# Moving the loads of the second expert behind its rows at the start of the expert stage

## The chip, the cores and the metric

The kernel runs on one core of a Trainium2 chip. That core has a matrix engine (TensorE, PE in the profile), a vector engine (VectorE, DVE), a scalar engine (ScalarE, ACT), a general engine (GpSimd, POOL) and a queue engine (SyncE, SP), which issues most of the transfers between the chip's large memory (HBM) and the on-chip memory. Each engine works through its own list of instructions in order and waits for the others at semaphores. The metric is the time of one execution on the device in microseconds (us); the times shown are medians of several runs of the same kernel.

## The reference

The reference computes three stages one after the other, in float32:

```
# 1. attention: batch 4, heads 8, sequence 576, head size 64
scores = q @ k.T / sqrt(64) + min(-(cum_i - cum_j), 0)   # cum: running sum of max(s, 0); causal mask
x = softmax(scores) @ v                                   # reshaped to 2304 rows of 512

# 2. mixture of experts: 8 experts, inner size 1024, one expert for each row
idx  = argmax(cosine(x, expert_emb) / tau)                # which expert a row goes to
gate = softmax(...)[idx]                                  # a row's own gate weight
out[idx == e] = gate * (max(x[idx == e] @ w1[e], 0) @ w2[e])

# 3. a gated product on all rows: inner size 1536
y = ((out @ w_a) * (out @ w_b)) @ w_out
```

Which expert a row goes to is known only once attention and routing are done.

## The kernel before, in words

Every matrix product is made of three products of float32r values: a number is split into a high part (a cast) and a low part (the number less its high part), and high by high, high by low and low by high are added up. So each weight block goes through a split after it has been loaded: ScalarE casts two halves (line 273, through `hi_op`), and VectorE and GpSimd subtract one half each (line 281, `lo_op`).

**Routing.** During attention each finished group of 128 rows is scattered by an indirect transfer of GpSimd (line 1046) into a buffer `xs` in HBM, where every expert has its own stretch of rows. The unused end of a stretch is zeroed by `zfill(e)` (line 1359, one transfer from `zrow`, issued at line 1257), and `xload(e)` (line 1364) fetches an expert's rows into the tile `xg` with two transfers (lines 1374 and 1375; for the first expert three, line 1372). `xs` is one tile to the framework: a fetch waits until the zeroing before it is done, and a zeroing waits until the fetch before it is done. There is one `xg` buffer.

**Expert stage.** Experts are taken in turn, e = 0 to 7, and each in eight steps f = 0 to 7. Step (e, f) (`products`, line 1592) makes the 128 hidden columns f (12 matmuls into the bank `h`, line 1553), and after them the share that step f - 1 has in the four output banks `y` (12 matmuls, line 1578). Behind the first of these, ScalarE makes the high part `hh` with the relu (line 1561) and VectorE the low part `hl` (line 1562); the second reads both one step later. From step 3 on, three transposes a step (`xtr`, line 1390, matmuls at line 1397) turn a quarter of the next expert's rows, for which these have to be there. At an expert's end `yout` (line 1585) copies the four banks to `mx` tiles and stores them to `yt` in HBM.

**Weights.** An expert has eight blocks of 512 KB, written here as (e, 0) to (e, 7): four of `w1` and four of `w2`. `wload2` (line 1423) issues the next block's load on SyncE, `wsplit2` (line 1429) splits the oldest loaded one. They are called at the end of each step, so that on ScalarE the casts of a step stand between the `hh` of this step and that of the next. Blocks (0, 0) to (0, 6) are loaded during attention.

**The passage from attention to the experts** (lines 1750 to 1775) is the place of the change. SyncE, after (0, 4) to (0, 6), issues the load of (0, 7); the counts of rows are read; the first expert's rows are fetched; meanwhile TensorE repeats matmuls with an unused result (`idle`, line 1754; its two counts are `WARM[2]` and `WARM[6]`), VectorE and GpSimd make the low parts of (0, 4) to (0, 6), and two of five small pieces of the gate weights (`misc`: m1 to m5, lines 1477 to 1511) are computed. Then come `zfill(1)`, three more loads, the transposes of the first expert's rows (`xtr0`, line 1377: eight for columns up to 256, four for the rest, each into a bank that ScalarE and VectorE have to have read), and the loop of steps. In it `xload(1)` stands in step (0, 1), and this step has two splits and two loads.

The order is that of the source text: within this part of the program nothing reorders the instructions of an engine. What SyncE waits for holds back every transfer behind it.

**Third stage.** `abmm(i, f)` (line 1633) makes 128 columns of both products of a group of 384 rows. ScalarE copies one to an `mx` tile (line 1649), VectorE multiplies it by the other (line 1654). `omm` (line 1688) makes the output products. `mx` tiles come from a pool of four (`mxp`, line 1342), which `yout` uses too. The last expert's `yout` falls between `abmm(0, 0)` and `abmm(0, 1)`.

Of the kernel before, what the change touches and what calls it, by code (L numbers as in the profile page):

```python
# [18 lines left out]
B, H, S, D = 4, 8, 576, 64  # L19
# [13 lines left out]
FIRST = float(1 << 20)  # L33
TICKS = (1, 1, 2)
PEND = (10, 1, 1)
WARM = (30, 84, 2, 0, 20, 10, 3)
LAT = 140.0
GATE = 3000.0
DRAIN = 93.0
# [1 line left out]
DEP = mybir.DependencyInfo(mybir.DependencyClass.Sync, mybir.DependencyReason.DATA)  # L41
# [103 lines left out]
def moe_kernel(tc, q, k, v, s, emb, tau, w1, w2, wa, wb, wo, out, dbg=None):  # L145
    nc = tc.nc
# [3 lines left out]
    left, right = ExitStack(), ExitStack()  # L150

    def pool(st, n, b, **kw):
        return st.enter_context(tc.tile_pool(name=n, bufs=b, **kw))
# [28 lines left out]
    with left, right:  # L182
# [38 lines left out]
        slots = {}  # L221
# [7 lines left out]
        def slot_src(e, j):  # L229
            return w1_src(e, j) if j < 4 else w2_src(e, j - 4)  # L230
# [6 lines left out]
            nslot[0] += len(spare)  # L237
            return (spare[0] if spare and x < 62 and (x + 3) % 5 > 2 else stage).tile(shape, dtype, name=nm, tag="st")

        def slot_load(src):  # L240
            t = slot([128, 1024], F32, "st")
            d = t if len(src.shape) == 2 else t.rearrange("p (a c) -> p a c", a=src.shape[1])
            nc.sync.dma_start(out=d, in_=src)
            return t

        def slot_load64(src):
# [32 lines left out]
        def lo_op(eng, t, o, a, b):  # L279
            e = nc.vector if eng == "D" else nc.gpsimd  # L280
            e.tensor_tensor(out=o[:, 1, a:b], in0=t[:, a:b], in1=o[:, 0, a:b].bitcast(F32), op=ALU.subtract)  # L281
# [7 lines left out]
        if True:  # L289
# [773 lines left out]
            wstate, wtok = {}, {}  # L1063
# [275 lines left out]
            gp = pool(mo, "gp", 1)  # L1339
            spare.append(pool(mo, "spare", 2))  # L1340
            hp = pool(right, "hp", 2, side="right")
            mxp = pool(right, "mxp", 4, side="right")
            keep = pool(right, "keep", 1, side="right")
            pos = keep.tile([128, NT], U32, name="pos")
            pd = keep.tile([128, NT, 2], F32, name="pd")
# [7 lines left out]
            def who(e):  # L1353

                if e not in pes:
                    pes[e] = nc.sync.value_load(ci[:1, 3, e:e + 1], min_val=0, max_val=E - 1) if e else 0
                return pes[e]
# [19 lines left out]
            def xtr0():  # L1377
                t = xhs[0] = [xhp.tile([128, 4, GT], F32R, name=x)[:, :, :CAPS[0]] for x in ("xh", "xl")]
                for a0, a1 in ((0, 256), (256, CAPS[0])):
                    for d in range(4):  # L1380
                        for a in range(a0, a1, 128):
                            nc.tensor.transpose(
                                out=yb[d][:, a:a + 128], in_=xgs[0][:, a // 128, 128 * d:128 * d + 128], identity=ident
                            )
                        nc.scalar.copy(out=t[0][:, d, a0:a1], in_=yb[d][:, a0:a1])
                        nc.vector.tensor_tensor(
                            out=t[1][:, d, a0:a1], in0=yb[d][:, a0:a1], in1=t[0][:, d, a0:a1].bitcast(F32), op=ALU.subtract
                        )

            def xtr(e, d):  # L1390
                if d == 0:
# [28 lines left out]
            def ringpool(nm):  # L1420
                return ringa0 if nm in ("w0", "w1", "w2", "w3") else rings[nm] if nm in rings else ringa1[0] if nm[0] == "w" else rings[nm[0]]

            def wload2():
                if loaded[0] < len(jobs):
                    key = jobs[loaded[0]][0]
                    stg[key] = slot_load(slot_src(who(key[0]), key[1]))
                    loaded[0] += 1

            def wsplit2():
# [325 lines left out]
                for x in range(n):  # L1755
                    warm((hb + yb)[x % 6], w[:, :128], w[:, :512], 1)

            wload2()
            idle(WARM[2])
            most = nc.values_load(cov[:1, 0:1], min_val=-CAP, max_val=N)  # L1760
            overflow()
# [2 lines left out]
            who(1)  # L1764
            idle(WARM[6])
            count(0)
            for j in range(4, 7):
                for x in range(2):
                    lo_op("DG"[j == 6], wstate[j], slots[0, j], 512 * x, 512 * x + 512)
            for _ in range(2):  # L1770
                misc.pop(0)()
            zfill(1)
            for _ in range(3):
                wload2()
            xtr0()
            prev = None
            for e in range(E):
                for f in range(8):
                    if f == 5 and e + 1 < E:
                        count(e + 1)  # L1780
                    products(e, f, prev)
                    prev = (e, f)
                    if (e, f) == (0, 1):
                        xload(1)
                    if (e, f) == (1, 0) or f == 7 and 0 < e < E - 2:
                        xload(e + 2 - (f == 0))
                    if (e, f) == (E - 2, 7):
                        yload(0)
                    if f == 4 and e + 2 < E:
                        zfill(e + 2)  # L1790
                    if 3 <= f < 7:
                        if e + 1 < E:
                            xtr(e + 1, f - 3)
                        else:
                            ysplit(0, f - 3)
                    if e == E - 1 and f == 7:
                        yload(1)
                    for _ in range(2 if (e, f) == (0, 1) else 1):
                        wsplit2()
                        wload2()  # L1800
                    if e == E - 2 and f >= 4:
                        vload()
                    if e == E - 1:
                        for _ in range(TICKS[0] if f not in (4, 6) else 0):
                            tick(5 if f < 4 else 3)
                    if misc and (e or f > 1):
                        misc.pop(0)()
# [74 lines left out]
```

## Time and profile before

| | |
|---|---|
| median of 3 runs | 956.17 us (954.9 to 956.58) |
| the profiled execution: its own time | 953.78 us |
| the profiled execution: span of the core | 952.1 us |
| TensorE busy | 917.8 us, 96% of the span |
| VectorE, ScalarE, GpSimd busy | 54%, 45%, 27% |
| mean granted clock of TensorE (profiled execution) | 0.994 of 2.4 GHz |
| transfers | 107.90 MB, mean 113 GB/s |

The span runs from the first to the last instruction in the trace; the execution's own time is 1.7 us longer, and the median of the runs 2.4 us longer than that. All clock times below count from the start of the span. A row of a timeline merges like instructions that follow each other: start, time until the last of them ends, engine, line, operation, destination and source; in square brackets the engine's idle time before it, and what ended that. Matmuls overlap in the pipeline, so the single times of a row add up to more than it lasts. The granted clock is 1.00 at 2.4 GHz and 0.50 at 1.2 GHz.

### The profile page before, as it was taken

The numbers are of one execution on the slowest core, as the hardware profiler recorded it, in microseconds if no ns is written. First come the engines' busy times: TensorE is split into PE (matmuls) and PEld (weight loads), VectorE is DVE, ScalarE is ACT, GpSimd is POOL, SyncE is SP. The second block draws the span as 40 slices with busy tenths as digits, with TensorE's granted clock in tenths as the row PEclk, the third lists the DMA queues.
The fourth block names the chain that finished last, engine by engine and source line by source line (L and its number), as shares of the span: only waits on it lengthen the run. The fifth ranks groups of instructions, "written<-read, shape, count | busy, mean of one in ns | idle before, by whom it ended". The sixth has DMA issues, their size and how long they took to land.

```text
span 952.1 us, 17669 instructions
## 1 busy us (share of the span) xinstructions
PE 917.8 (96%) x6447; PEld 839.7 (88%) x6448; DVE 516.9 (54%) x1319; ACT 432.0 (45%) x1074; POOL 256.4 (27%) x308
## 2 busy tenths in 40 slices
PE   8998999999889999999999999999999999999996
PEld 7777878777669999999998999999999999999995
DVE  8788888798756343455678888732212222222112
ACT  6677888876645444455544434421211111121111
POOL 6122323256234333344303344632001001001001
PEclk9999999999999999999999999999999999999999
DMA  5774555526277667677736444412010010000000
GB/s 136 175 154 105 143 116 123 140 71 185 96 221 241 225 193 218 215 226 241 223 106 204 129 118 131 90 26 75 1 34 34 1 34 34 1 1 34 1 1 34
DMA packets 102259, 107.90 MB, mean 113 GB/s; under 512 B 58445, under 2 KB 72733, under 8 KB 102157
## 3 DMA queue, kind: packets, MB, share of 16 engines
q1 hardware_dynamic: 98573, 97.04, 36.0%
q0 software_dynamic: 3552, 9.46, 2.8%
q8 instruction: 65, 1.06, 0.5%
q14 instruction: 37, 0.30, 0.1%
q10 hardware_dynamic: 32, 0.04, 0.0%
HBM read 77.90 MB, written 20.44 MB: 103 GB/s over the span
## 4 chain that ended last, share of the span: by engine, by line
PE 68%; DMA 2%; DVE 0%; issue 0%; SPq 0%; POOLq 0%; ACT 0%; DVEq 0%; ACTq 0%
PE h L1643 16%; PE x L1643 16%; PE y L1664 14%; PE y L1578 10%; PE h L1553 10%; DMA xg<-xs 1%; PE x L1397 1%; PE x L1664 1%; PE h L1664 1%; DMA xs<-zrow 1%; DMA yt<-mx 0%; DVE xl L1631 0%; SPq L1372 0%; POOLq L1878 0%; DVE mx L1654 0%
## 5 line engine op out<-in xcount | busy, mean ns | idle before, releaser
L1654 DVE TENSOR_TENSOR mx<-x,mx 128x384 f32<-128x384 f32 x72 | 39.9, 555 | 225.1 <-PE x L1643 225.0
L1655 ACT CAST hh<-mx 128x384 fp32r<-128x384 f32 x71 | 36.4, 512 | 159.0 <-DVE mx L1654 159.0
L1649 ACT COPY mx<-h 128x384 f32<-128x384 f32 x72 | 34.5, 479 | 150.8 <-PE h L1643 149.8
L1683 POOL DMA_INDIRECT out_dram<-mx,pmt x18 | 17.6, 979 | 292.5 <-DVE mx L1682 223.2
L653 ACT ACTIVATE z<-z,mn 128x192 f32<-128x192 f32 (+3 forms) x128 | 78.2, 611 | 37.9 <-DVE mn L647 37.2
L1643 PE MATMUL h<-xh,w 128*128 128x384 f32 x288 | 79.8, 337 | 1.3 <-ACT mx L1649 1.3
L1643 PE MATMUL h<-xh,v 128*128 128x384 f32 x288 | 79.7, 337 | 0.0
L1643 PE MATMUL x<-xh,w 128*128 128x384 f32 x288 | 78.9, 334 | 0.0
L633 PE MATMUL st<-KS,QS 128*128 128x288 f32 (+3 forms) x160 | 58.7, 374 | 9.4 <-DVE mn L647 7.4
L756 PE MATMUL pt<-ident,z 128*128 128x128 f32 x448 | 63.5, 277 | 3.3 <-ACT pT L180 1.6
L281 POOL TENSOR_TENSOR w<-st,w 128x512 fp32r<-128x512 f32 (+1 forms) x43 | 47.1, 1101 | 68.1 <-ACT w L273 57.8
L647 DVE CUSTOM_DVE_ANT_0 z<-st,maskb 128x192 f32<-128x192 f32 (+3 forms) x128 | 58.7, 477 | 9.5 <-PE st L636 7.3
L1562 DVE SCALAR_TENSOR_TENSOR hl<-h,hh 128x288 fp32r<-128x288 f32 (+6 forms) x64 | 31.2, 487 | 58.8 <-ACT hh L1561 58.8
L1656 DVE TENSOR_TENSOR hl<-mx,hh 128x384 fp32r<-128x384 f32 x71 | 39.7, 559 | 41.1 <-ACT hh L1655 41.1
L800 PE MATMUL xa<-pT,vn 128*64 128x128 f32 x896 | 60.0, 278 | 1.9 <-ACT pT L180 1.6
L281 POOL TENSOR_TENSOR v<-st,v 128x512 fp32r<-128x512 f32 x32 | 43.2, 1353 | 62.5 <-ACT v L273 48.7
L1664 PE MATMUL y<-v,hh 128*128 128x512 f32 x192 | 59.8, 392 | 0.0
L756 PEld LDWEIGHTS pt<-ident,z 128*128 128x128 f32 x448 | 49.9, 141 | 11.0 <-ACT z L653 4.3
L1553 PE MATMUL h<-xh,v 128*128 128x256 f32 (+2 forms) x256 | 59.0, 304 | 0.0
L1578 PE MATMUL y<-hh,v 128*128 128x256 f32 (+2 forms) x256 | 58.0, 300 | 0.0
L1553 PE MATMUL h<-xh,w 128*128 128x288 f32 (+3 forms) x256 | 57.8, 302 | 0.0
L800 PEld LDWEIGHTS xa<-pT,vn 128*64 128x64 f32 x896 | 47.9, 137 | 11.0 <-issue 5.6
(308 smaller groups left out, 2520.0 us busy)
## 6 DMA issues: line engine op xcount, KB each, us to landing
st<-in_moe_w_dram SPq DMA_DIRECT2D x64, 512.0 KB
QS<-sp SPq DMA_DIRECT2D x62, 128.0 KB
st<-in_moe_w_a_dram SPq DMA_DIRECT2D x12, 512.0 KB
st<-in_moe_w_b_dram SPq DMA_DIRECT2D x12, 512.0 KB
st<-in_moe_w_out_dram SPq DMA_DIRECT2D x12, 512.0 KB
xg<-yt SPq DMA_DIRECT2D x6, 768.0 KB
xg<-xs SPq DMA_DIRECT2D x7, 512.0 KB
kn<-in_k_dram SPq DMA_DIRECT2D x24, 128.0 KB
```

The source lines that it names most:

```text
L281: e.tensor_tensor(out=o[:, 1, a:b], in0=t[:, a:b], in1=o[:, 0, a:b].bitcast(F32), op=ALU.subtract)
L633: nc.tensor.matmul(st[:m, :wp], lhsT=qs[:, h, s0 - 64:s0 - 64 + m], rhs=ks[:, h, c0:c0 + wp], start=True, stop=False)
L647: nc.vector.tensor_tensor_reduce(out=z[:m, h, c0:c0 + w], in0=st[:m, :w], in1=maskb[:m, S - kk + c0:S - kk + c0 + w], op0=ALU.add, op1=ALU ...
L653: nc.scalar.activation(out=z[:m, h, :kk], in_=z[:m, h, :kk], func=AF.Exp, scale=-1.0, bias=m1, accum_out=rsum[:m, tid(b, c), 2 * p + h:2 * ...
L756: nc.tensor.transpose(out=pt[:, 128 * x:128 * x + 128], in_=zs[i][:, h, a0:a0 + 128] if c else z0s[u % 2], identity=ident)
L800: nc.tensor.matmul(xa[64 * h:64 * h + 64, :m], lhsT=v_[:m, 2 * p + h, :], rhs=locs[i][bk, h], start=bk == 0, stop=bk == c,)
L1553: nc.tensor.matmul(ph[:, :n], lhsT=w[:, hl, 128 * f:128 * f + 128], rhs=mv[:, d, :n], start=k_ == 0, stop=k_ == 11,)
L1578: nc.tensor.matmul(ys[e][d][:, :n], lhsT=w[:, hl, c0 + 128 * d:c0 + 128 * d + 128], rhs=mv[:, :n], start=f == 0 and k_ == 0, stop=f == 7 a ...
L1643: nc.tensor.matmul(p, lhsT=w[:, hl, d, c0:c0 + 128], rhs=mv[:, d, :], start=d == 0 and k_ == 0, stop=d == 3 and k_ == 2,)
L1654: nc.vector.tensor_tensor(out=g, in0=pp[1], in1=g, op=ALU.mult)
L1656: nc.vector.tensor_tensor(out=gl, in0=g, in1=gh.bitcast(F32), op=ALU.subtract)
L1664: nc.tensor.matmul(ots[i][t], lhsT=st[:, 128 * t:128 * t + 128], rhs=w[:, hl, c0:c0 + 512], start=f == 0 and k_ == 0, stop=f == 11 and k_ ...
```

## The change

There are four edits; the loads of the first two steps are laid out anew with the first and the third.

- The load of (0, 7) moves from ahead of the passage to behind the call of `xtr0`, and gets a wait of its own: it is issued once the ninth transpose of the first expert's rows (the first of the second group) is done. `zfill(1)` stands behind it. Only one more load, (1, 0), is issued ahead of the loop instead of three.
- The `idle` counts go from 2 and 3 to 1 and 2. Piece m3 of the gate weights (an exponential with its table load on ScalarE) joins m1 and m2 in the passage, and so m4 and m5 move up a step. The low parts of (0, 5) go from VectorE to GpSimd.
- `xload(1)` moves from step (0, 1) to step (0, 0). In step (0, 0) there is one split and two loads, in step (0, 1) two of each; after it the loads stand three blocks ahead of the splits, where it was four.
- The pool of `mx` tiles grows from four to five.

```
-WARM = (30, 84, 2, 0, 20, 10, 3)
+WARM = (30, 84, 1, 0, 20, 10, 2)
...
-        def slot_load(src):
+        def slot_load(src, after=None):
...
-            nc.sync.dma_start(out=d, in_=src)
+            x = nc.sync.dma_start(out=d, in_=src)
+            if after:
+                tc.add_manual_dep(x.ins, after, DEP, reason="rows first")
...
-            mxp = pool(right, "mxp", 4, side="right")
+            mxp = pool(right, "mxp", 5, side="right")
...
+                        if a0 and d == 0:
+                            first = x.ins.name
+                return first
...
-            wload2()
             idle(WARM[2])
...
-            for j in range(4, 7):
+            for x in range(2):
+                lo_op("D", wstate[4], slots[0, 4], 512 * x, 512 * x + 512)
+            for _ in range(3):
+                misc.pop(0)()
+            for j in (5, 6):
                 for x in range(2):
-                    lo_op("DG"[j == 6], wstate[j], slots[0, j], 512 * x, 512 * x + 512)
-            for _ in range(2):
-                misc.pop(0)()
+                    lo_op("G", wstate[j], slots[0, j], 512 * x, 512 * x + 512)
+            turned = xtr0()
+            wload2(turned)
             zfill(1)
-            for _ in range(3):
-                wload2()
-            xtr0()
+            wload2()
...
-                    if (e, f) == (0, 1):
+                    if (e, f) == (0, 0):
                         xload(1)
...
-                    for _ in range(2 if (e, f) == (0, 1) else 1):
-                        wsplit2()
+                    for x in range(2 if e == 0 and f < 2 else 1):
+                        if f or x == 0:
+                            wsplit2()
                         wload2()
```

What stands on SyncE in a row, before: from the zeroing of the second expert's rows (`xs<-zrow`) to the end of the fetch of its rows (`xg<-xs`). The four loads `st<-in_moe_w1` are the blocks (1, 0) to (1, 3); `ISA` rows work out an address.

```order
L1257 DMA xs_95<-zrow_270 736x1x256
L1537 UNCONDITIONAL_BRANCH x3
L243 ISA
L243 DMA st_4885<-in_moe_w1_dram 128x1024
L243 ISA
L243 DMA st_4887<-in_moe_w1_dram 128x1024
L243 ISA
L243 DMA st_4889<-in_moe_w1_dram 128x1024
L243 ISA
L243 DMA st_4955<-in_moe_w1_dram 128x1024
L1374 ISA
L1374 DMA xg_5010<-xs_95 128x2x512
```

And now, at the same place on SyncE: the first load is block (0, 7), which waits for the ninth transpose; the two loads `st<-in_moe_w1` are (1, 0) and (1, 1).

```order
L243 DMA st_4911<-in_moe_w2_dram 128x2x512
L1259 ISA
L1259 DMA xs_95<-zrow_270 736x1x256
L1542 UNCONDITIONAL_BRANCH x3
L243 ISA
L243 DMA st_4914<-in_moe_w1_dram 128x1024
L1376 ISA
L1376 DMA xg_4945<-xs_95 128x2x512
L1377 ISA
L1377 DMA xg_4945<-xs_95 112x512
L243 ISA
L243 DMA st_4953<-in_moe_w1_dram 128x1024
```

The zeroing now has the load of (0, 7) ahead of it, and the load of (1, 1) now stands behind the fetch of the rows, which waits for the zeroing.

What stands on ScalarE in a row, before, from the relu of step (0, 0) to that of step (0, 3) (`hh`); the casts `w7`, `v0`, `v1`, `v2` are the splits of (0, 7), (1, 0), (1, 1), (1, 2), and the table load with `lt` is m3.

```order
L1561 ACTIVATE hh_4946<-h0_4631 128x352
L273 CAST w7_4950<-st_4637 128x512 x2
L1537 UNCONDITIONAL_BRANCH
L1561 ACTIVATE hh_5006<-h1_4632 128x352
L1537 UNCONDITIONAL_BRANCH
L273 CAST v0_5013<-st_4885 128x512 x2
L273 CAST v1_5020<-st_4887 128x512 x2
L1561 ACTIVATE hh_5076<-h0_4631 128x352
L273 CAST v2_5080<-st_4889 128x512
L1537 UNCONDITIONAL_BRANCH
L273 CAST v2_5080<-st_4889 128x512
L1488 ACT_TABLE_LOAD
```

And now, the same piece on ScalarE:

```order
L1566 ACTIVATE hh_4941<-h0_4631 128x352
L275 CAST w7_4948<-st_4911 128x512 x2
L1542 UNCONDITIONAL_BRANCH
L1566 ACTIVATE hh_5006<-h1_4632 128x352
L1542 UNCONDITIONAL_BRANCH
L275 CAST v0_5010<-st_4914 128x512 x2
L275 CAST v1_5017<-st_4953 128x512 x2
L1566 ACTIVATE hh_5073<-h0_4631 128x352
L275 CAST v2_5077<-st_4955 128x512
L1542 UNCONDITIONAL_BRANCH
L275 CAST v2_5077<-st_4955 128x512
L1566 ACTIVATE hh_5137<-h1_4632 128x352
```

The table load has left this place; the casts of (1, 1) stand ahead of the relu of step (0, 2), as they did.

## Rows read from the trace of the kernel before

**Rows 1.** The page, part 1: busy time of each engine

```profile
PE 917.8 (96%) x6447; PEld 839.7 (88%) x6448; DVE 516.9 (54%) x1319; ACT 432.0 (45%) x1074; POOL 256.4 (27%) x308
```

**Rows 2.** Waits of TensorE from 285 on: us in total, times, longest

```profile
PE h L1643 <- ACT mx L1649: 1.3, 1, 1.3
PE x L1397 <- DMA xg<-xs: 0.3, 1, 0.3
```

**Rows 3.** The chain that ended last, 240 to 330: start, us, what

```profile
266.21 3.38 DMA xg<-xs
...
269.80 6.20 DMA xs<-zrow
...
276.73 8.23 DMA xg<-xs
```

**Rows 4.** Timeline of TensorE, and of its weight loads (PEld), in the passage

```profile
269.27 0.75 PEld L1382 LDWEIGHTS y<-ident,xg 128*128 128x128 f32 x7 [0.67 <-DMA xg<-xs]
...
270.57 1.32 PE L1382 MATMUL y<-ident,xg 128*128 128x128 f32 x4 [0.31 <-DVE xl L1386]
...
281.26 0.30 PE L1578 MATMUL y<-hh,w 128*128 128x288 f32 x1
...
284.27 0.41 PE L1397 MATMUL x<-ident,xg 128*128 128x128 f32 x2 [1.25 <-DMA xg<-xs]
...
285.12 0.39 PE L1553 MATMUL h<-xh,w 128*128 128x288 f32 x1
```

**Rows 5.** Timeline of SyncE, the issue of transfers

```profile
234.94 9.45 SPq L243 DMA_DIRECT2D st<-in_moe_w_dram  x3
...
270.67 4.64 SPq L243 DMA_DIRECT2D st<-in_moe_w_dram  x4
276.11 0.39 SPq L1374 DMA_DIRECT2D xg<-xs  x1
```

**Rows 6.** Timeline of ScalarE in the passage

```profile
269.68 2.48 ACT L1385 CAST xh<-y 128x256 fp32r<-128x256 f32 x8 [6.75 <-issue]
...
279.19 1.14 ACT L273 CAST v<-st 128x512 fp32r<-128x512 f32 x2 [0.37 <-DMA st<-in_moe_w_dram]
280.24 0.46 ACT L1561 ACTIVATE hh<-h 128x352 fp32r<-128x352 f32 x1
...
281.74 1.28 ACT L1488 ACT_TABLE_LOAD   x1
```

**Rows 7.** Timeline of VectorE and of GpSimd in the passage

```profile
280.73 0.53 DVE L1562 SCALAR_TENSOR_TENSOR hl<-h,hh 128x352 fp32r<-128x352 f32 x1
...
275.13 1.30 POOL L281 TENSOR_TENSOR w<-st,w 128x512 fp32r<-128x512 f32 x1 [11.27 <-ACT w L273]
```

**Rows 8.** Transfers, 250 to 300: how much the zeroing moves

```profile
xs<-zrow SPq DMA_DIRECT2D x1, 736.0 KB
```

**Rows 9.** Windows: stretch, length, PE busy, granted clock, DMA share, GB/s

```profile
271.00:272.00 1.00, 1.00 (x5) 1.00 0.78 172
272.00:273.00 1.00, 1.00 (x10) 1.00 0.92 187
...
276.00:277.00 1.00, 1.00 (x10) 1.00 0.98 385
```

**Rows 10.** Windows, the same columns, around two waits of TensorE

```profile
262.00:264.50 2.50, 0.00 (x0) 1.00 0.04 10
...
265.00:268.00 3.00, 3.00 (x5) 0.50 0.59 158
...
283.00:284.20 1.20, 0.03 (x1) 1.00 1.05 265
```

**Rows 11.** Timelines behind the last expert's stores: ScalarE, TensorE, VectorE

```profile
502.47 0.48 ACT L1649 COPY mx<-h 128x384 f32<-128x384 f32 x1 [1.07 <-DMA yt<-mx]
...
503.00 0.44 PE L1643 MATMUL h<-xh,w 128*128 128x384 f32 x1 [1.25 <-ACT mx L1649]
...
503.44 0.55 DVE L1654 TENSOR_TENSOR mx<-x,mx 128x384 f32<-128x384 f32 x1
```

More of the change, by code (lines that the diff above doesn't have):

```diff
@@ L1381, in xtr0 @@
                         for a in range(a0, a1, 128):
-                            nc.tensor.transpose(
+                            x = nc.tensor.transpose(
                                 out=yb[d][:, a:a + 128], in_=xgs[0][:, a // 128, 128 * d:128 * d + 128], identity=ident
@@ L1421, in ringpool, with wload2 @@
                 return ringa0 if nm in ("w0", "w1", "w2", "w3") else rings[nm] if nm in rings else ringa1[0] if nm[0] == "w" else rings[nm[0]]
-            def wload2():
+            def wload2(after=None):
                 if loaded[0] < len(jobs):
                     key = jobs[loaded[0]][0]
-                    stg[key] = slot_load(slot_src(who(key[0]), key[1]))
+                    stg[key] = slot_load(slot_src(who(key[0]), key[1]), after)
                     loaded[0] += 1
```

## The prediction

> **What bounds the kernel now.** Read the busy times first: TensorE is busy 96% of the span, the next engine 54% [rows 1]. So an edit pays only where TensorE stands still, and costs only where it makes TensorE stand still. The waits of TensorE name the places: from 285 us to the end there are two rows, 0.3 us for the second expert's rows and 1.3 us behind a copy of ScalarE [rows 2]; the expert stage is otherwise a closed row of matmuls. The chain of waits shows what leads up to the first place: the first expert's rows land 3.38 us after the last of their three issues, at 269.59; then the zeroing, issued at 269.80, takes 6.20 us, to 276.00; then the second expert's rows take from 276.73 to 284.96 [rows 3]. The timeline of TensorE has the stall itself: the product y of step (0, 2) starts at 281.26 and lasts about 1.6 us, the three transposes stand at 284.27 behind 1.25 us of idle time, and step (0, 4) starts at 285.12 [rows 4]. About 2.1 us go there.
>
> Now see how near another wait lies. The casts of block (1, 1) start at 279.19, held by their load (0.37 us of idle time before them); behind them come hh of step (0, 2), from 280.24 [rows 6], and hl, from 280.73 for 0.53 us, to 281.26 [rows 7]. That is when TensorE starts the y that reads them [rows 4]. It did not wait, but there was nothing to spare: whatever makes block (1, 1) later makes this y later by the same.
>
> **Part by part.**
>
> *Load of (0, 7).* Before, it is the third of the three issues that end at 244.39 [rows 5], 20 us ahead of anything that needs the queue: it cost nothing there. Now it waits for the ninth transpose, which starts at 270.57 [rows 4]; with 0.33 us for it (four such steps in 1.32 us) SyncE goes on at 270.9. The zeroing, issued at 269.80 before, comes after this issue (0.39 us for one, as that of the rows [rows 5]) and its own address, at about 271.5: 1.7 us later. The transfers add to that. The 736 KB of the zeroing [rows 8] go at 187 GB/s, though four loads were issued from 270.67 on, and the loads come behind it at 385 GB/s [rows 5, 9]: SyncE's transfers run one behind the other, so 512 KB ahead of the zeroing hold it for 524,288 B / 385 GB/s = 1.4 us. Its data took 753,664 B / 187 GB/s = 4.0 of its 6.20 us; with the transfer engines 0.78 busy in the window from 271 to 272 and 0.92 in the next [rows 9] they began near 271.1, 1.3 us after the issue, which leaves 0.9 us from the last byte until it is told done. Then (0, 7) moves from 270.9 + 1.3 = 272.2 to 273.6, the zeroing from 273.6 to 277.6, and it is done at 278.5, 2.5 us later than before. Bounds: +1.7 (issue alone) to +3.0.
>
> *Rows one step sooner.* The fetch used to stand behind four loads, now behind one, but its wait is the zeroing, which was the last to end before too. Issues at 278.6 and 279.2 (0.1 and 0.7 after the zeroing, as before). About 1.3 us later it moves, 736 KB (the second expert's 368 rows of 2 KB) at 265 GB/s [rows 10], 2.8 us, to 282.7, and lands near 283.3. TensorE would want the rows at 282.9: this wait is all but gone.
>
> *What is late next.* All that stood ahead of the fetch stands behind it: SyncE in its wait holds (1, 1), (1, 2), (1, 3). Block (1, 1) is issued at 279.7, moves behind the rows from 282.7 to 284.1 and, with 0.9 us to be told done, can be cast at 285.0, against 279.19: +5.8. By the chain above y of step (0, 2) then starts at 281.26 + 5.8 = 287.1, TensorE idle since 281.3. Add 1.6 us for y and 0.3 for the transposes (their rows are there): step (0, 4) starts at 289.0 against 285.12, **+3.9 us**. Bounds: with the zeroing only 1.7 later, (1, 1) issued at 278.9, and 3.4 us from issue to landing (the rows of the first expert from their last issue [rows 3]), the cast is at 282.3 and the term +1.1; at the upper end +4.5.
>
> *Clock.* TensorE had no work from 262.0 to 264.5, and in the next 3 us of matmuls, 265 to 268, the granted clock stood at 0.50, the 1.2 GHz level; after the 1.25 us at 283 it was still at 1.00 [rows 10]. The new wait, 5.8 us, is longer than either, so I take a like stretch of half clock behind it: 3.2 us of matmuls that at 2.4 GHz would take half, **+1.6 us**. Bounds 0 and +1.8. The Trainium skill, "TensorE: Matmul & The Clock Gate", section "HAM oscillation — how this bites in real kernels", speaks against the change here: bursts of matmuls that follow a long enough wait for data each begin at half rate. By it the term stands, without it the sum below is 1.6 us less; the trace has it once, in the row at 0.50.
>
> *Five mx tiles.* ScalarE's copy at 502.47 waited 1.07 us for a store of `yt` that had the tile, and TensorE's 1.25 us at 503.00 hang on this copy [rows 11]. With a fifth tile the copy of `abmm(0, 1)` gets the one that `abmm(0, 0)` used. It moves up by 1.07, and so does the product h. The next product x needs VectorE's multiply, 503.44 to 503.99 [rows 11]; h then ends at 501.93 + 2.1 = 504.0, just clear. **-1.1 us**; bounds -1.3 and 0 (the multiply is late instead).
>
> *At nothing.* Fewer idle matmuls: the second transpose waited 0.67 us for rows [rows 4], so TensorE is early anyway; if the clock falls for it, see the last rival. m3 in the passage: ScalarE sat idle 6.75 us there [rows 6]; the table load that goes from 281.74 stands behind the relu that decides. Without that cover it would cost its 1.28 us plus the exponential. The low parts of (0, 5) on GpSimd, two of 1.30 us: they are in its idle 11.27 us [rows 7], and first read at 281. m4 and m5 a step sooner stand on VectorE ahead of hl of steps (0, 3) and (0, 4), at most some 0.3 us, while these steps are late anyhow. One load less in advance: still three steps, 10 us, for 1.4 us of data; 0 to +0.5.
>
> *Sum.* 3.9 + 1.6 - 1.1 = +4.4 us. On the profiled execution's own 953.78 that is 958.2; the median of the runs shown lies 2.4 us above it, and the time compared is a median, so 956.17 + 4.4 = **960.6 us**. The ends: 1.1 + 0 - 1.3 = -0.2 and 4.5 + 1.8 + 0.5 = +6.8, 956.0 to 963.0.
>
> **Rivals.**
>
> *Late block, full clock.* The stall as above, but the clock stays at 1.00 through it, as through the stall at 283: 956.17 + 3.9 - 1.1 = 959.0.
>
> *Short zeroing.* What would let block (1, 1) through is a zeroing that is done sooner. The Trainium skill, "DMA: Bandwidth & Descriptors", section "Anatomy of one DMA — SWDGE (gpsimd) path", fits 2.0 us plus the bytes at 436 GB/s to a transfer; for 753,664 B my estimate from it is 3.7 us, and the sum by it would be 2.5 us less. The trace has 6.20 us for this very transfer, and the measurement decides. The mechanism in rows alone: the 6.20 us hold part of the wait for a busy memory, which is emptier now, and rows and loads mix instead of queueing, so that (1, 1) is cast at the lower bound, 282.3. Then +1.1 and -1.1 cancel: 956.2, no change. Against it: the zeroing ran alone at 187 GB/s and had nothing to wait for.
>
> *Faster.* The rows' wait goes and nothing takes its place: -2.1 at 283, -1.1 at 503, so 953.0. For it, the rows' wait is the largest left in this stage, and the edits go straight at it. It decides from (1, 1) being castable by 279.2; with the zeroing done after 277.7 even at its lower bound, and the block issued behind that, the trace has no way to this, unless ScalarE's list let the relu past the casts, which it doesn't.
>
> *Cold passage.* With one idle matmul less before the rows, the half clock of 265 to 268 goes on through the transposes and the first products, and makes the ninth transpose, on which the new chain hangs, later too: another 1.6 us, 962.2.
>
> **How the numbers follow.** Late block with half clock 0.46 (960.6, by itself 958.5 to 962.5), with full clock 0.20 (959.0), cold passage 0.08 (962.2), short zeroing 0.14 (956.2), faster 0.12 (953.0). A measurement of this kernel can tell about 0.2%, 1.9 us, from no change. The first three lie over 958.1, less 0.02 for their lower edge: slower 0.72. Short zeroing with that edge: same 0.16. Faster 0.12. The range goes from 955.5, so that short zeroing is in, to 963.0, the upper end of the sum; outside are the faster case and a few hundredths above.
>
> **What would show it.** Right: in the profile after, TensorE has a wait of 4 to 6 us for the hh or hl of the first expert between 281 and 288, in place of the wait for rows; the casts of (1, 1) wait for their load until about 285; the fetch of the second expert's rows is issued near 278.6; a stretch of granted clock at 0.50 follows; the copy at 502 waits for no store. Wrong: casts of (1, 1) before 281, or the zeroing done before 277, or a fetch that lands after 285 and is still what TensorE waits for.

## The result, and the profile after

The changed kernel takes 962.32 us in the median of five runs (961.38 to 965.02), the kernel before 954.9 beside it (953.97 to 956.58): ratio 1.0077, 95% interval 1.0064 to 1.009, 7.4 us slower. The forecast was 960.6 in a range of 955.5 to 963.0; its sum was +4.4. The profiled execution took 963.86 us, span 962.2.

The page, part 1, answers [rows 1]: TensorE has 3.6 us more busy time in a span that is 10.1 us longer.

```profile
PE 921.4 (96%) x6443; PEld 843.0 (88%) x6444; DVE 517.9 (54%) x1317; ACT 431.8 (45%) x1074; POOL 259.3 (27%) x310
```

The waits of TensorE from 285 on (total, times, longest), against [rows 2]: one row of another kind has taken the place of both.

```profile
PE y L1583 <- ACT hh L1566: 4.6, 1, 4.6
```

The chain that ended last, 240 to 330, against [rows 3]. It no longer goes through the second expert's rows but through a weight block: zeroing, fetch, `st` (block (1, 1)), its cast, the relu, y of step (0, 2).

```profile
268.34 5.17 DMA xg<-xs
...
276.05 6.98 DMA xs<-zrow
...
283.16 0.39 SPq L1376
...
283.78 0.33 SPq L1377
...
284.30 5.74 DMA st<-in_moe_w_dram
...
291.62 3.57 PE y L1583 x12
295.19 0.64 PE x L1402 x3
295.82 1.68 PE h L1558 x12
```

Timeline of SyncE, against [rows 5]: (0, 7), the zeroing, (1, 0), then 5.8 us of nothing until the fetch may go, and behind it six loads in one group, (1, 1) first.

```profile
275.22 0.40 SPq L243 DMA_DIRECT2D st<-in_moe_w_dram  x1
276.05 0.66 SPq L1259 DMA_DIRECT2D xs<-zrow  x1
276.92 0.46 SPq L243 DMA_DIRECT2D st<-in_moe_w_dram  x1
283.16 0.39 SPq L1376 DMA_DIRECT2D xg<-xs  x1
...
284.30 8.67 SPq L243 DMA_DIRECT2D st<-in_moe_w_dram  x6
```

Timeline of ScalarE, against [rows 6]: the casts of (1, 1) wait 4.38 us for their load and end where hh, the third row, begins.

```profile
284.54 1.14 ACT L275 CAST v<-st 128x512 fp32r<-128x512 f32 x2 [3.34 <-DMA st<-in_moe_w_dram]
290.06 1.14 ACT L275 CAST v<-st 128x512 fp32r<-128x512 f32 x2 [4.38 <-DMA st<-in_moe_w_dram]
291.11 0.46 ACT L1566 ACTIVATE hh<-h 128x352 fp32r<-128x352 f32 x1
```

Timeline of TensorE, against [rows 4]: the first idle matmul, the second group of them, the ninth transpose, the stall, and step (0, 4).

```profile
261.54 1.81 PE L174 MATMUL h<-w 128*128 128x512 f32 x2 [0.76 <-DVE jk L1303]
268.32 3.75 PE L174 MATMUL h<-w 128*128 128x512 f32 x4 [4.97 <-PEq L1709]
...
274.86 1.47 PE L1384 MATMUL y<-ident,xg 128*128 128x128 f32 x4 [0.32 <-DVE xl L1388]
...
291.62 0.61 PE L1583 MATMUL y<-hh,w 128*128 128x288 f32 x1 [4.60 <-ACT hh L1566]
...
295.48 0.58 PE L1558 MATMUL h<-xh,w 128*128 128x288 f32 x1
```

Windows of the changed kernel (stretch, length, PE, PEld, DVE, ACT and POOL busy, granted clock, DMA share, GB/s): the first products, the stall, y of (0, 2) with its transposes, and what follows. Half clock stands at the first and behind the stall.

```profile
275.50:278.60 3.10, 3.10 (x14) 2.93 (x14) 1.14 (x5) 0.71 (x3) 0.00 (x0) 0.50 0.64 202
...
289.10:291.60 2.50, 0.00 (x0) 0.00 (x0) 0.69 (x2) 1.54 (x4) 0.32 (x1) 0.50 1.03 393
291.60:295.80 4.20, 4.18 (x16) 3.90 (x17) 3.57 (x7) 1.35 (x3) 2.57 (x2) 0.50 0.97 347
296.00:297.00 1.00, 1.00 (x10) 1.00 (x9) 0.64 (x2) 1.00 (x3) 0.00 (x0) 1.00 0.93 216
```

And behind the last expert's stores, against [rows 11], ScalarE's copy waits for no store and TensorE's 1.25 us are gone:

```profile
511.99 0.47 ACT L1654 COPY mx<-h 128x384 f32<-128x384 f32 x1
...
512.51 0.44 PE L1648 MATMUL h<-xh,w 128*128 128x384 f32 x1
```

The attention stage ends at another time in every execution (the first idle matmul, with unchanged code ahead of it, at 258.25 in the profile of before and 261.54 here), so spans can't be subtracted. This table counts from that matmul, all from the timelines of TensorE, in us; the last column is the start of the transposes of step (0, 7).

```
                                first   y of    step    transposes
                                h       (0, 2)  (0, 4)  of (0, 7)
before                          13.44   23.01   26.87   37.11
before, again (9)               14.05   23.62   25.78   36.03
five mx tiles (1)               13.13   22.70   26.24   36.48
changed                         14.45   30.08   33.94   44.37
changed, again (5)              13.20   28.33   31.97   42.21
(0, 7) early (2)                13.71   25.59   27.96   38.78
fetch behind (1, 1) (3)         13.12   24.42   28.19   40.39
busy stall (4)                  13.66   30.56   32.78   43.03
both undone (6)                 14.69   24.27   26.10   37.13
blocks in the row wait (7)      14.31   23.88   25.72   38.67
more idle matmuls (8)           14.04   31.28   35.14   45.75
both undone, fewer idle (10)    13.45   23.03   24.85   36.91
wide zeros, changed (11)        13.34   28.54   32.40   43.24
wide zeros, before (12)         14.47   24.05   26.22   36.46
```

Before and changed, two profiles each, differ by (44.37 + 42.21 - 37.11 - 36.03) / 2 = 6.7 us at the last column and by 0.1 at the first h: the loss lies within the first expert's steps.

### The profile page after: what moved, and what is told of

The parts are those of the page before. It is cut to its first block, busy times and chain, and to the rows that moved or that the text cites. A ratio compares the mean times of both kernels' runs of the same rounds, so it can differ in the third digit from the quotient of the medians.

```text
span 962.2 us, 17650 instructions
## 1 busy us (share of the span) xinstructions
PE 921.4 (96%) x6443; PEld 843.0 (88%) x6444; DVE 517.9 (54%) x1317; ACT 431.8 (45%) x1074; POOL 259.3 (27%) x310
## 4 chain that ended last, share of the span: by engine, by line
PE 68%; DMA 2%; DVE 1%; issue 0%; ACT 0%; SPq 0%; POOLq 0%; ACTq 0%; DVEq 0%
PE h L1648 16%; PE x L1648 15%; PE y L1669 14%; PE y L1583 11%; PE h L1558 10%; PE x L1402 1%; PE x L1669 1%; PE h L1669 1%; DMA xs<-zrow 1%; DMA st<-in_moe_w_dram 1%; DMA xg<-xs 1%; DVE xl L1636 0%; POOLq L1885 0%; PE y L1384 0%; DVE cv L268 0%
## 5 line engine op out<-in xcount | busy, mean ns | idle before, releaser
L283 POOL TENSOR_TENSOR w<-st,w 128x512 fp32r<-128x512 f32 (+1 forms) x45 | 50.5, 1131 | 67.2 <-ACT w L275 53.2
L1583 PE MATMUL y<-hh,w 128*128 128x288 f32 (+3 forms) x256 | 57.9, 302 | 4.6 <-ACT hh L1566 4.6
```

The lines of the kernel that those rows point to most:

```text
L1583: nc.tensor.matmul(ys[e][d][:, :n], lhsT=w[:, hl, c0 + 128 * d:c0 + 128 * d + 128], rhs=mv[:, :n], start=f == 0 and k_ == 0, stop=f == 7 a ...
```

## The experiments

The first ten ran where the kernel before itself takes 970 to 971 us, the last two where it takes 955.5; each is compared with the kernel before beside it. Experiments 8 and 9 are one run each and have no ratio.

**1. Five mx tiles alone**, on the kernel before.

```diff
-            mxp = pool(right, "mxp", 4, side="right")
+            mxp = pool(right, "mxp", 5, side="right")
```

> The kernel before with one edit: the pool mxp has five buffers and no longer four. Theory (the fifth buffer takes the wait of ScalarE's copy for a store away): 1.1 us faster than before, ratio 0.9988; ScalarE's copy near 502 us waits for no store, TensorE's 1.25 us ahead of h near 503 is gone or under 0.2 us. Rival (VectorE's multiply, which frees the bank of the next product, is late instead): 0 to 0.2 us, and a wait for it stands near 503 in the place of the old one.

Ratio 1.0, interval 0.9983 to 1.0017: no gain shown, 1.1 us not excluded. The copy waits for no store, but it doesn't in experiment 9 either, with four tiles. The 1.07 us of [rows 11] come and go with the landing of a store.

**2. (0, 7) ahead of the row wait again**, all else changed.

```diff
+            wload2()
             idle(WARM[2])
...
-            turned = xtr0()
-            wload2(turned)
             zfill(1)
             wload2()
+            xtr0()
```

> The changed kernel with the load of (0, 7) put back ahead of the row wait, so that the zeroing no longer stands behind it and behind the ninth transpose; all else as changed. Theory (the zeroing is late by the wait for the transpose, and block (1, 1) hangs on the zeroing): zeroing issued about 2.5 us sooner as seen from the last row transposes, TensorE's wait for hh of step (0, 2) falls from 4.6 to about 2 us, time 2.5 us below the changed kernel (959.8 us; ratio to before 1.005), and up to 2.3 us less again (957.5) if the granted clock then stays at 1.00 behind the shorter wait. Rival (the block is late by its place behind the fetch alone, and the zeroing's own start is hidden by the queue): within 0.5 us of the changed kernel, the wait still 4 us or more.

Ratio 1.0039 (1.002 to 1.0058). The stall is 1.57 us:

```profile
294.65 1.14 ACT L275 CAST v<-st 128x512 fp32r<-128x512 f32 x2 [3.73 <-DMA st<-in_moe_w_dram]
```

```profile
296.20 0.40 PE L1583 MATMUL y<-hh,w 128*128 128x288 f32 x1 [1.57 <-ACT hh L1566]
```

The late zeroing is real: without it step (0, 4) starts 4.0 us sooner than in experiment 5 (31.97 to 27.96): y of (0, 2) starts 2.7 us sooner, and at full clock it takes 1.3 us less to step (0, 4). What is left is the fetch ahead of the block: its casts start 24.04 us from the first idle matmul, against 20.94 before, +3.1.

**3. The fetch behind (1, 1)**, (0, 7) and zeroing as changed: `xload(1)` moves from ahead of step (0, 0)'s two loads to behind the first of them.

```diff
-                    if (e, f) == (0, 0):
-                        xload(1)
...
                         wload2()
+                        if e + f + x == 0:
+                            xload(1)
```

> The changed kernel with one call moved: in step (0, 0) the fetch of the second expert's rows is issued behind the loads of (1, 1) and (1, 2) and no longer ahead of them; (0, 7) and the zeroing stay as changed. Theory (SyncE in the fetch's wait for the zeroing holds block (1, 1)): the casts of (1, 1) start about 4 us sooner, 3.2 us after the zeroing is done as in the kernel before; the wait of TensorE falls from 4.6 to under 1 us, the half clock behind it goes too, and the time is 4 to 6 us below the changed kernel, 956 to 958.4 us, most likely 957. The rows land later, near 5 us after the zeroing, and TensorE doesn't wait for them, or under 0.5 us. Rival (the zeroing itself, behind (0, 7) and the transposes, is what makes the block late, whatever the order): within 1 us of the changed kernel. Second rival (the fetch takes the block's place as the late one): the wait for hh goes, one for the rows of 3 us or more comes, time 960 to 962.

The edit does less than the text above says: only (1, 1) is now issued ahead of the fetch, and (1, 2) still stands behind it. Ratio 1.0029 (1.001 to 1.0048), 2.8 us over before and so below the changed kernel's 1.0059 by some 2.9 (the two intervals overlap): less than the 4 to 6 of the theory. Step (0, 4) comes 3.8 us sooner than in experiment 5 (28.19), but the stall is still 1.56 us: (1, 0) and (1, 1) are issued behind the late zeroing, and hh starts 23.91 us from the first idle matmul, 1.9 later than before. The casts of (1, 2) then wait 3.33 us, and later steps are late: from step (0, 4) to the transposes of (0, 7) it takes 12.2 us, against 10.24 before.

```profile
289.14 2.36 ACT L275 CAST v<-st 128x512 fp32r<-128x512 f32 x4 [4.43 <-DMA st<-in_moe_w_dram]
291.41 0.46 ACT L1566 ACTIVATE hh<-h 128x352 fp32r<-128x352 f32 x1
295.19 1.14 ACT L275 CAST v<-st 128x512 fp32r<-128x512 f32 x2 [3.33 <-DMA st<-in_moe_w_dram]
```

**4. TensorE kept busy in the stall**: nine idle matmuls ahead of y of (0, 2).

```diff
+                    xb = bank("x") if (e, f) == (0, 3) else None
                     def both(n):
                         mm(n)
+                        if xb is not None:
+                            warm(xb, w[:, :128], w[:, :512], 9)
                         mm2(n)
```

> The changed kernel with nine idle matmuls (into the x bank that is free, results unused) between h of step (0, 3) and y of step (0, 2), where TensorE stood still for 4.6 us. They add no work that anything waits for, only keep TensorE busy. Theory (the wait leaves TensorE at the 1.2 GHz level for the 6.8 us behind it, and that costs about 2.3 us on top of the wait): granted clock at 1.00 through y of (0, 2) and h of (0, 4), y of (0, 2) in about 1.6 us and no longer 3.57, time 2 to 2.5 us below the changed kernel, 960 us. Rival (the clock falls there whatever TensorE does, or the idle matmuls run past the wait): no gain or up to 3 us slower, y of (0, 2) still at half speed.

Windows, the idle matmuls in the first two, y of (0, 2) and h of (0, 4) in the third: clock 1.00 throughout.

```profile
291.40:295.00 3.60, 3.60 (x11) 1.69 (x10) 0.00 (x0) 0.00 (x0) 1.11 (x1) 1.00 0.90 307
295.00:298.70 3.70, 3.70 (x10) 1.55 (x10) 2.45 (x5) 2.89 (x6) 2.01 (x2) 1.00 0.98 384
298.70:302.60 3.90, 3.90 (x29) 3.66 (x28) 2.67 (x6) 1.38 (x3) 0.87 (x1) 1.00 0.98 306
```

From y of (0, 2) to step (0, 4) it takes 2.22 us, against 3.64 and 3.86 in the two profiles of the changed kernel: the clock costs 1.4 to 1.6 there, and 0.2 more in h of (0, 4) in the first. The time itself is no better (1.0056): hh was there at 296.88, and the idle matmuls ran until 298.72, 1.8 us too long. The mechanism is shown, the gain not.

**5. The changed kernel again.** No edit.

> The changed kernel once more, beside the runs of the kernel before on the chip of the first four experiments, whose attention stage takes some 8 us longer from run to run. Theory (the passage and the stall behind it carry the whole loss): counted from the first idle matmul, step (0, 4) starts near 34 us and no longer near 27, 7 us later than before; TensorE waits 4 to 5 us for hh of step (0, 2); the ratio to before is 1.006 to 1.008. Rival (a part of the 7.4 us that the medians gave was the attention stage's own, which ended 3.3 us later in the one profiled run): step (0, 4) 4 us later, ratio 1.004.

Ratio 1.0059 (1.0038 to 1.008), 5.7 us. The chain has the same links; the third row is y at half clock.

```profile
282.16 6.97 DMA xs<-zrow
...
290.40 5.26 DMA st<-in_moe_w_dram
...
297.23 3.56 PE y L1583 x12
```

```profile
295.68 1.14 ACT L275 CAST v<-st 128x512 fp32r<-128x512 f32 x2 [3.86 <-DMA st<-in_moe_w_dram]
```

The casts start at 26.78 from the first idle matmul, 5.84 later than before, and y waits 5.40 us. Step (0, 4) starts at 31.97, 5.1 and 6.2 us behind the two profiles of before, where 7 was expected.

**6. Both undone**: the edits of 2 and 3 together, and 2 and 3 idle matmuls.

```diff
-WARM = (30, 84, 1, 0, 20, 10, 2)
+WARM = (30, 84, 2, 0, 20, 10, 3)
```

> The changed kernel with three edits undone: (0, 7) is loaded ahead of the row wait, so the zeroing starts as early as before; the fetch stands behind the loads of (1, 1) and (1, 2), though still a step sooner than before and ahead of (1, 3); the idle matmuls are 2 and 3 again. Five mx tiles, gate weights and low parts stay as changed. Theory (the casts of (1, 1) start 3 us late by the fetch ahead of them and 4.4 us late by the late zeroing, and nothing else in the change costs anything): no wait for hh or hl over 0.3 us, and the rows land with no or one block less ahead of them, so that TensorE waits for them under 0.5 us; step (0, 4) starts at 25 to 26 us from the first idle matmul, against 26.9 before; 1 to 3 us faster than before, ratio 0.997 to 0.999. Rival (some other part, the gate weights on ScalarE or the low parts of (0, 5) on GpSimd, holds the passage): 2 us or more slower than before, with a wait for ScalarE or VectorE ahead of the first product.

Ratio 1.0008 (0.9992 to 1.0024): the loss is gone, the gain of the theory is not there. The low parts of (0, 5) and the gate weights stay as changed here, so they are not what the changed kernel loses. No wait for hh or rows up to step (0, 4): it starts 11.41 us from the first h, against 13.43 in the first profile of before and 11.73 in experiment 9, which has no wait for rows either. So 2.0 us are won against the one and 0.3 against the other. The first h is 1.25 and 0.64 us later than in these two, since the idle matmuls (granted clock 0.50 until 280.9) hold TensorE past the rows, and 0.8 us go again behind step (0, 4). Timeline of TensorE:

```profile
275.55 3.75 PE L174 MATMUL h<-w 128*128 128x512 f32 x4 [3.03 <-PEq L1709]
279.09 1.92 PE L174 MATMUL y<-w 128*128 128x512 f32 x2
280.80 1.20 PE L1384 MATMUL y<-ident,xg 128*128 128x128 f32 x8
```

**7. (1, 0) and (1, 1) loaded in the row wait**, on the kernel before with five mx tiles; the fetch right behind the zeroing.

```diff
+            for _ in range(2):
+                wload2()
             zfill(1)
-            for _ in range(3):
-                wload2()
             xtr0()
...
-                    if (e, f) == (0, 1):
+                    if (e, f) == (0, 0):
                         xload(1)
...
```

What is left out are the splits and loads of the first two steps, laid out as in the changed kernel.

> The kernel before with five mx tiles and another order on SyncE: the loads of (1, 0) and (1, 1) right behind the first expert's rows and ahead of the zeroing, the fetch right behind the zeroing, then (1, 2) and (1, 3). Theory (SyncE's transfers run one behind the other, so what stands ahead of the zeroing no longer waits for it, and what stands behind it does): the casts of (1, 0) and (1, 1) wait for no load after 279 us on the clock of the kernel before; the zeroing is done 1.4 us later at most, the rows land 1 to 3 us sooner since four loads no longer stand between; TensorE's wait for them is under 0.5 us, step (0, 4) starts at 24.8 to 25.5 us from the first idle matmul; 2 to 3.2 us faster than before, ratio 0.9967 to 0.998. Rival (the two loads share the transfer engines with the first expert's rows): the row transposes start 1 to 2.7 us later and the kernel is no faster, or up to 1.5 us slower.

Ratio 1.0011 (0.9998 to 1.0025), no faster. The blocks are cast without a wait and step (0, 4) starts at 25.72, but now (1, 2) is the one behind the fetch; its casts wait 4.61 us, a table load follows them, and y of (0, 3) waits:

```profile
294.51 1.14 ACT L273 CAST v<-st 128x512 fp32r<-128x512 f32 x2 [4.61 <-DMA st<-in_moe_w_dram]
...
295.67 1.28 ACT L1488 ACT_TABLE_LOAD   x1
...
297.70 0.40 PE L1578 MATMUL y<-hh,w 128*128 128x288 f32 x1 [1.65 <-ACT hh L1561]
```

**8. The idle matmuls alone undone**, on the changed kernel (the edit of `WARM` in 6).

> The changed kernel with the idle matmuls around the row wait at 2 and 3 again, a look without timing. Theory (one idle matmul less on either side leaves TensorE at half clock in the first products, which took 4.5 us and no longer 3.3): h of steps (0, 0) and (0, 1) take 3.3 us together, and step (0, 4) starts 1.3 us sooner from the first idle matmul than in the changed kernel (32.6 instead of 33.9), TensorE still waiting 4 to 5 us for hh. Rival (the half clock in these products comes and goes from run to run, since two of three experiments with the same idle matmuls as the changed kernel had 3.25 us): nothing is shown by one look either way, and the wait for hh takes up what the products gain, since the block's time doesn't hang on them.

The first two h take 3.25 us here, but so they do in experiments 3, 4 and 5 with fewer idle matmuls. Step (0, 4) starts at 35.14, no sooner: y hangs on the block, and TensorE waits 7.5 us for it. The half clock in the first products cost the changed kernel nothing; the stall took it up.

**9. The kernel before.** No edit.

> The kernel before, one look, on the chip of the experiments, which had no profile of it yet. Theory (this chip adds its time outside the passage): counted from the first idle matmul, the first product h starts at 13.1 to 13.4 us and step (0, 4) at 26.2 to 26.9 us, as in the first profile of before and with five mx tiles; TensorE waits 1 to 1.3 us for the second expert's rows; the stall of 5 to 6.5 us near 630 to 640 us that all experiments have and the two first profiles don't is there too, so it is the chip's and no edit's. Rival (the edits brought that stall): it is absent, and every ratio above holds it.

The late stall is there, in pieces: 2.5 + 1.0 + 0.9 + 0.6 = 5.0 us between 600 and 660 (waits of TensorE).

```profile
PE y L1664 <- issue: 2.5, 3, 1.0
PE h L1664 <- issue: 1.0, 3, 0.3
PE x L1643 <- issue: 0.9, 1, 0.9
PE x L1664 <- issue: 0.6, 1, 0.6
```

The wait for rows is not: the first h is 0.6 us later than in the first profile of before, and the rows land 1.1 us sooner (25.62 and 26.71 from the first idle matmul). So the 2.1 us at 283 that the change goes at are not there in every run.

**10. Both undone, with fewer idle matmuls**: experiment 6 with `WARM` as changed.

> The sixth experiment with the idle matmuls 1 and 2, as in the changed kernel. There six idle matmuls at the 1.2 GHz level ran until 12.25 us from the first, past the rows, and the transposes started at 12.04; with five or four ahead they started at 9.6 to 11. Theory (at half clock the idle matmuls hold TensorE past the rows): first product h at 13.1 to 13.7 us and no longer 14.69, step (0, 4) at 24.6 to 25.4 (26.10 there), with no wait for hh, hl or rows over 0.3 us; 1 to 3 us faster than before, ratio 0.997 to 0.999. Rival (fewer idle matmuls bring a half clock into the transposes and first products, as in the first profile of the changed kernel): the 24 matmuls of h of steps (0, 0) and (0, 1) take 4 us or more and no longer 3.25, first product no sooner, same time as before or slower.

Ratio 1.0004 (0.9989 to 1.0019), no faster. The first h is at 13.45 and step (0, 4) at 24.85, the earliest of all; then y of (0, 3) waits 1.54 us for hl. Two things together make hl late: the casts of (1, 2), whose load stands behind the fetch, wait 2.98 us (first row, ScalarE), and on VectorE the gate weights (`gm`), a step sooner than before, take 1.7 us between the low part of this block and hl:

```profile
292.72 1.14 ACT L275 CAST v<-st 128x512 fp32r<-128x512 f32 x2 [2.98 <-DMA st<-in_moe_w_dram]
...
293.98 0.31 DVE L1496 TENSOR_REDUCE gm<-lt 128x20 f32<-128x160 f32 x1
294.32 0.94 DVE L1497 TENSOR_SCALAR gm<-gm 128x20 f32<-128x20 f32 x1
295.30 0.28 DVE L1498 RECIPROCAL gm<-gm 128x20 f32<-128x20 f32 x1
295.61 0.18 DVE L1499 TENSOR_TENSOR pd<-gm 128x20 f32<-128x20 f32 x1
295.70 0.52 DVE L1567 SCALAR_TENSOR_TENSOR hl<-h,hh 128x352 fp32r<-128x352 f32 x1
```

**11 and 12. The zeroing in 2 KB pieces**, on the changed kernel, and on the kernel before with five mx tiles.

```diff
-            zrow = rt.tile([128, DM // 2], F32, name="zrow")
+            zrow = rt.tile([128, DM], F32, name="zrow")
...
+                k = 1 if x == 1 else 2
...
-.rearrange("(p a c) -> p a c", p=16, c=DM // 2)
+.rearrange("(p a c) -> p a c", p=16, c=DM // k)
...
-[:, 0].unsqueeze(1).to_broadcast([16, CAPS[x] // 8, DM // 2])
+[:, 0, :DM // k].unsqueeze(1).to_broadcast([16, CAPS[x] * k // 16, DM // k])
```

> The changed kernel with the zeroing of the second expert's rows written in pieces of 2 KB and no longer 1 KB: the same 736 KB from the same 16 partitions in 368 pieces and no longer 736; the source tile is twice as wide. Theory (the zeroing goes at 187 GB/s because of the size of its pieces, and block (1, 1) hangs on its end): the zeroing takes 4 to 5.5 us from issue to landing and no longer 6.2 to 7, TensorE's wait for hh of step (0, 2) is 1.5 to 2.5 us shorter than in the three profiles of the changed kernel (4.6, 5.4, 7.5 us), and the time 1 to 2.5 us less: ratio to before 1.003 to 1.0055. Rival (16 partitions or the memory set its rate, not the pieces): zeroing still 6 us or more, wait and ratio as in the changed kernel, 1.0059.

> The kernel before with five mx tiles and the same wide zeroing. Theory: the zeroing done 1 to 2 us sooner, the casts of (1, 0) and (1, 1) and the second expert's rows with it; no wait for rows (1.1 to 1.3 us in two of three profiles with the old zeroing), step (0, 4) at 12.0 us from the first product h (13.4, 13.1 and 11.7 there); 0 to 1.5 us faster than before, ratio 0.9985 to 1.0. Rival (rate set by partitions or memory): zeroing 6.2 us as before, ratio 1.0 within its interval and the wait for rows as it was.

In the changed kernel: ratio 1.0061 (1.0041 to 1.0082), the stall 5.47 us, the zeroing 0.4 us shorter:

```profile
273.21 6.58 DMA xs<-zrow
```

Halving the number of pieces has little effect: on the kernel before, too, it takes 5.93 us from the issue of the zeroing to that of the fetch behind it, against 6.31. What sets the rate was not found. On the kernel before: ratio 0.9983 (0.997 to 0.9995), 1.6 us faster, the only version shown to be faster than before. TensorE has no wait for rows in it and none at all from 285 to the end, but its passage is also a late one, as in experiment 9 (first h at 14.47); which part each edit has in the 1.6 us is open.

## Why the prediction was right, and where its sizes were off

**Right.** TensorE waits for hh of step (0, 2) where that was said, for the reason that was said. The second profile of the changed kernel meets the working step by step, counted from the first idle matmul: zeroing issued 1.7 us later than before (said 1.7), done at 20.2 (said 20.25), fetch at 20.36 (20.35), (1, 1) issued at 21.50 (21.45), cast at 26.78 (26.75). The other profiles of this order spread around it: y of (0, 2) was said for 28.85, and starts at 28.33 there, at 30.08 in the first profile, 31.28 in experiment 8 and 28.54 in experiment 11. Experiments 2 and 3 part the 5.8 us: the fetch ahead alone makes 3.1, the late zeroing alone 1.9, and together they make 0.8 more than these two.

**Half clock behind the wait.** Said 1.6; experiment 4 shows 1.4 to 1.6 in y and its transposes, 0.2 more in h once. The Trainium skill, "TensorE: Matmul & The Clock Gate", section "HAM oscillation — how this bites in real kernels", has bursts of matmuls that follow a long enough wait for data begin at half rate. The traces agree behind the waits of 4.6, 5.4, 5.5 and 7.5 us (the first profile, experiments 5, 11 and 8), where the clock stood at 0.50. With 1.6 us it went both ways: after experiment 2's wait the clock stayed at 1.00, after experiment 3's it was 0.65 on average over 3.8 us.

**Five mx tiles, -1.1: true of one pair of profiles, not of the other.** In the first pair it came as said. Counted from the first idle matmul, h of `abmm(0, 1)` is 7.4 us later than before (506.00 against 495.33), h of `abmm(1, 0)`, which had waited behind the copy, only 6.2 (512.51 against 503.00):

```profile
495.33 0.34 PE L1643 MATMUL h<-xh,w 128*128 128x384 f32 x1
...
506.00 0.34 PE L1648 MATMUL h<-xh,w 128*128 128x384 f32 x1
```

But it was no fixed cost: in experiments 5 and 9 the difference is 6.1 us at both places, since experiment 9 doesn't have the wait with four tiles, and by itself the edit shows no gain where the kernel takes 971 us (it was not run alone where it takes 955). A single profile had been read as a constant. Without this term the sum is +5.5, and the ratio beside experiment 5 gives +5.7.

**The other 2 us of the first result.** Its profile has the ninth transpose 1.0 us later than before (13.32 and 12.32 from the first idle matmul), where experiment 5 has it 0.25 sooner (12.07), and the load of (1, 1) takes 5.74 us and not 5.26: 1.25 + 0.48 = 1.73, the very difference of the two y (30.08 - 28.33 = 1.75). Why its rows landed 5.17 us after their last issue and no longer 3.38 is open; experiment 5 has 3.91. This is one execution: the intervals of the two ratios, 1.0064 to 1.009 and 1.0038 to 1.008, overlap, so the two results need not differ by more than noise.

**Gains at nothing.** The rows' wait went as said. That it is absent in one of two profiles of before makes this gain smaller than the 2.1 us that the stall was charged against. The gate weights on VectorE, set at nothing under cover of late steps and at some 0.3 us at most, are hidden here, but they take 1.7 us; without the stall they make TensorE wait 1.5 us, together with the late block (1, 2) (experiment 10).

**Rivals.** Cold passage: the half clock in the first products did come in the first profile, but in five of six others with the same idle matmuls they take 3.25 us (3.83 in experiment 2), and where it came it cost nothing: it is not what the idle matmul's removal does. Late block with full clock: refuted by the windows. Short zeroing: 6.97 us against 6.20, longer, not shorter. By the Trainium skill, "DMA: Bandwidth & Descriptors", section "Anatomy of one DMA — SWDGE (gpsimd) path", it would be 3.7 by my estimate. That section speaks of transfers that GpSimd issues, and this one is SyncE's; even with 2 KB pieces 6.58 were measured, so the measurement decides. Faster: in experiments 6, 7 and 10 TensorE waits neither for rows nor for (1, 1), and they are still no faster than before: 7 and 10 meet block (1, 2), which the fetch holds back, and 6 starts its first products later.

## What to carry to other kernels

An instruction that waits at the head of a queue is charged with everything behind it: before a fetch is moved up, write down what it passes, when each of these is due, and how long the fetch itself may have to wait. When one order of a queue after another leaves some transfer late (here the rows, then (1, 1), then (1, 2)), look at what the queue waits for, here the zeroing, before another order; that this pays is not shown, the 2 KB pieces took only 0.4 us off it. And take a wait of one microsecond from two profiles before counting on its removal.

## What the runs showed of the hardware that was not expected

SyncE's zeroing takes 0.6 to 0.8 us longer with one 512 KB load issued just ahead (6.77 to 6.98 in four profiles, against 6.13 to 6.21 in four without). That much the prediction's sum has too, 7.0 us from issue to done: by that sum a part of the load's own 1.4 us passes before the zeroing would have begun to move. Not expected was that in experiments 1 to 10, the kernel before among them, TensorE lost 4.8 to 6.7 us between 625 and 646 us. For most of it the profile shows no releaser; in experiments 1, 2 and 10 about half is a wait for VectorE's multiply. The two first profiles and the last two have nothing there.
